# Attention with two feed-forward layers: early weights decoded over ten steps a piece, bias groups behind the steps' own work, first products amid the end

## The chip, the cores and the metric

One core of one Trainium2 chip runs the kernel as one program. The metric is the device time of one execution in microseconds; a kernel's time is the median of its runs. The engines are named as in the profile: PE (TensorE, with PEld for its weight loads), DVE (VectorE), ACT (ScalarE), POOL (GpSimd) and SP, whose queue issues all DMAs of this kernel.

## What is computed

```python
scores = scale * q @ k.T                      # 4 batches, 8 heads, 576 positions, 64 wide
x = (log1p(|i - j|) / log1p(max(i, 1)))[..., None]
scores = scores + (relu(x @ w1 + b1) @ w2)    # a bias per head, from an MLP of 32 hidden units
attn = softmax(scores)                        # with 1e-9 added to the sum
x = attn @ v                                  # reshaped to 2304 tokens x 512
h = x @ w_in; x = (h - tanh(h)) @ w_out       # 512 -> 2048 -> 512
x = (silu(x @ w_gate) * (x @ w_val)) @ w_out2 # 512 -> 1536 -> 512
```

The feed-forward products are exact to more than one pass gives: each operand is split into a high and a low part, and a product is three matmuls (`matmul3`, L681). The weights are given as 8 byte numbers and are decoded on the chip into such a pair.

## The kernel before

**Bias groups.** The bias is made in 36 groups (`bias_rows`, L145): four Relu rows (`bias_hidden`, L127, three on DVE L140 and one on ACT L142, made one group ahead), eight matmuls on PE, one eviction on ACT with a scale, and one DMA to a scratch array in DRAM. When the groups of a span t of 128 positions are done, `bias_load` (L178) reads them back as bias tiles, from a count of groups later on, and at once behind the last group. `GEN0` groups are made first, then `GEN_EACH` at a time while more than `GEN_LATE` are left; so 33 are made ahead of the units, and three in the units' first two steps.

**Units.** A unit is (pair of heads hp, batch b, span t); 16 pairs (hp, b), each of five spans in the order 4, 3, 2, 1, 0, give 80 steps. Step i works on several units at once, and the order of the letters in `FIRST_ORDER` (the first step of a pair), `STEP_ORDER` (the other four) and `END_ORDER` (three steps behind the last unit) is the order of issue on every engine. The letters: L loads of q, k, v on SP; u takes the unit of step i - 3 as the turn; C score matmuls (L302, two PSUM buffers, each freed by S); S the score reduction on DVE (L317, adds the bias tile and finds the maximum); E the exponentials on ACT (L328); N the reciprocals of the sums of unit i - 1 (L337, L338, DVE); M their scaling of the probabilities (L346, POOL); p and P transposes of the turn's probabilities (PE); F and D their copies out of PSUM (F on ACT L394 and L396, D on DVE L394 to L398); V products with v (L413, PE); X and Y the high and low part of x (xh on ACT L422, xl on DVE L428); Q, q, O, o transposes of the next pair's q and k and their copies; H and T the split of q and k (ACT L268, POOL L59); G one bias group.

**End.** `AV_END` gives the step at which the last pair's two groups of value products are issued: behind step 80 all of group 0, behind step 82 all of group 1. Each end step has two turns; behind each end step `aside` (L957) issues one item's hidden products of the first layer (`hidden`, 12 matmuls), and in the second also the first item's pointwise work and the planning of weights.

**Early weights.** A piece of weights is a 512 KB raw tile. While the units run, five pieces are decoded, and two more are begun. Eight operations make one piece, over three rounds: a (L626, DVE), b (L628, DVE), r (L615, ACT) and F (L632, POOL; another F than the copy above) for the piece that is first; m (L619, ACT) and W (L638, DVE, behind it the next raw DMA) for the second; h (L643, ACT) and l (POOL L59) for the third. `ALONE_PARTS` says which are issued in which step of a round: five steps a round, so the last 35 steps hold seven rounds, behind each step's own work.

```python
STEP_ORDER = "LuXYCHGGSTPpNMVFED"
ALONE_PARTS = ("ma", "", "bhW", "rl", "F")
if 0 <= left < 5 * (EARLY_PAIRS + 2):
    weights.part_of_step(-1, (4 - left) % 5)
```

**After the units** come 140 items of the two layers in one loop; item i's hidden products are issued ahead of the output products of item i - 2, with the pointwise work of i on ACT, DVE and POOL between.

Of the kernel before, what the change touches and what calls it, by code (L numbers as in the profile page):

```python
# [17 lines left out]

B, H, S, D = 4, 8, 576, 64
HID = 32  # L20
NT, DM = B * S, H * D
FF1, FF2 = 2048, 1536
# [13 lines left out]
C_B1, C_W2 = C_W1 + 1, C_W1 + 2  # L36
NCONST = C_W2 + QG * H

# [6 lines left out]
    ((6, (0, 1)), (7, (2, 3, 4))),  # L45
    ((9, (0, 1, 2)), (10, (3, 4))),
)
AV_END = {(0, 0): (5, (0, 1, 2, 3, 4)), (1, 0): (7, (0, 1, 2, 3, 4))}

FIRST_ORDER = "LuCpQGGSOPqNMVFoED"  # L50
STEP_ORDER = "LuXYCHGGSTPpNMVFED"
END_ORDER = "NMuPpFDuPpFDVXY"

LAG = 3
GEN_ORDER = [G for t in TORDER for G in range(8 * t, min(8 * t + 8, NG))]
# [6 lines left out]
class Attention:  # L62
# [34 lines left out]
    def bias_setup(self):  # L97
# [17 lines left out]
        for j in range(4):  # L115
            for g in range(QG):
# [3 lines left out]
                )  # L120
        self.scratch = [self.dram.tile([n * H, S], F32, name=f"bias_{t}") for t, (_, n) in enumerate(SPANS)]

# [55 lines left out]
    def bias_load(self, hp, t):  # L178
# [3 lines left out]
        )  # L182
        src = self.scratch[t].rearrange("(q h) k -> q h k", h=H)

# [247 lines left out]
    def run(self, early, aside):  # L432
# [6 lines left out]
        self.ps_qk = {}  # L439
        NP = H // 2  # L440
        units = [(hp, b, t) for hp in range(NP) for b in range(B) for t in TORDER]
# [17 lines left out]
        def gen(n):  # L459
            for _ in range(n):  # L460
                if gens:
                    G = gens.pop(0)
                    self.bias_rows(G)
                    done = NG - len(gens)
                    if not any(x // 8 == G // 8 for x in gens):
                        due.append((G // 8, done + 2))
                    if due and done >= due[0][1]:
                        self.bias_load(0, due.pop(0)[0])
                    if not gens:
                        for t, _ in due:  # L470
                            self.bias_load(0, t)
                        self.gen_ctx.close()
                        early()
# [17 lines left out]
        for n, (hp, b) in enumerate(pairs):  # L491
            for z, when in enumerate(AV_STEPS):
                for after, cs in when:
                    if (hp, b) == pairs[-1]:
                        after, cs = AV_END.get((z, cs[0]), (0, ()))
                    if cs:
# [17 lines left out]
        def transposes(which):  # L514
            return lambda i: i in preps and self.qk_transpose(*preps[i], which)

        at = lambda f, i: f(units[i]) if 0 <= i < len(units) else None
        last = len(units) - 1
# [5 lines left out]
        def next_turn(i):  # L524
# [6 lines left out]
            E=lambda i: at(self.expo, i), V=products, X=lambda i: self.values_high(), Y=lambda i: self.values_low(),  # L531
            Q=transposes("q"), q=transposes("k"), O=lambda i: self.qk_raw("q"), o=lambda i: self.qk_raw("k"),
            H=lambda i: i % 5 and self.qk_high(), T=lambda i: i % 5 and self.qk_low(), G=lambda i: gen(1),
        )
        for i in range(len(units) + 3):
            for a in END_ORDER if i > last else STEP_ORDER if i % 5 else FIRST_ORDER:
                work[a](i)
            if i == len(units) - 1:
                self.ps_ctx.close()
            if i >= len(units):  # L540
                self.values_high()
                self.values_low()
            aside(len(units) - 1 - i)
        self.values_high()
        self.values_low()

# [7 lines left out]
class Weights:  # L554
# [109 lines left out]
    def part_of_step(self, now, n):  # L664

        if n == 0:
            self.plan(now)
        for part in ALONE_PARTS[n]:
            dict(
# [19 lines left out]
SHARED_TWO = dict(s2=("two0", 0), g=("two0", 1), gh=("two1", 0), gl=("two1", 1))  # L689
GROUP1, GROUP2 = 4, 3  # L690
EARLY_PAIRS = 5
BEV_BUFS, GEN0, GEN_LATE, GEN_EACH = 5, 5, 4, 2
RAW_BUFS, POINT_AT = 2, -2
PACED, SOON = 74, 7
ALONE_PARTS = ("ma", "", "bhW", "rl", "F")
UNITS = [(0, 512), (512, 512), (1024, 512), (1536, 512), (2048, 256)]
ORDER, LAST_ORDER = (0, 1, 4, 2, 3), (0, 1, 2, 3, 4)

# [238 lines left out]
@with_exitstack  # L937
def moe_attention_kernel(ctx, tc, q, k, v, packed, w_in, w_out, w_gate, w_val, w_out2, out, dbg=None):
    nc = tc.nc
    xp = ctx.enter_context(tc.tile_pool(name="xp", bufs=1, side="right"))  # L940
    xh = xp.tile([128, 4, NT], F32R, name="xh")
    xl = xp.tile([128, 4, NT], F32R, name="xl")
    shared = ctx.enter_context(tc.tile_pool(name="shared", bufs=1))
    moe = Moe(tc, xh, xl, w_in, w_out, w_gate, w_val, w_out2, out, shared)
    weights = Weights(tc, moe.pieces)
    n1, n = moe.n1, len(moe.items)
    with tc.manual_schedule():
        with ExitStack() as ctx_a:
            moe.constants(shared)
            att = Attention(tc, (q, k, v, packed), xh, xl, shared)  # L950

            def early():
                weights.tmp_pools(ctx, "right")
                weights.pools(ctx, EARLY_PAIRS, "right")
                weights.load()

            def aside(left):  # L957

                if 0 <= left < 5 * (EARLY_PAIRS + 2):
                    weights.part_of_step(-1, (4 - left) % 5)  # L960
                if left < 0:
                    moe.matmuls(-1 - left)
                if left == POINT_AT:
                    weights.plan(0)
                    moe.pointwise(0, weights, True)

            att.pools(ctx_a)
            att.run(early, aside)
        if dbg and "xh" in dbg:
            nc.sync.dma_start(out=dbg["xh"], in_=xh.bitcast(F32))  # L970
            nc.sync.dma_start(out=dbg["xl"], in_=xl.bitcast(F32))
        weights.pools(ctx, 12 - EARLY_PAIRS, "left")
        weights.polite = False
        accp = ctx.enter_context(tc.tile_pool(name="acc", bufs=1))
        acc = accp.tile([128, 4 * NT], F32, name="acc")
        moe.acc = [acc[:, NT * j:NT * j + NT] for j in range(4)]
        moe.acc2 = [acc[:, 512 * j:512 * j + 512] for j in range(NT // 128)]
        moe.pools(ctx)
        held = []
        for i in range(n + 2):  # L980
            if 3 <= i < n:
                moe.matmuls(i)

            now = []
            if i >= 2:
                held.append(i - 2)
                if i >= n or i == 2 or not moe.starts(i - 2) or len(held) > 1:
                    now, held = held, []
            for j in now[:-1]:
                moe.out_matmuls(j)  # L990
            if 1 <= i < n:
                weights.plan(i)
                moe.pointwise(i, weights, i == n - 1)
            for j in now[-1:]:
                moe.out_matmuls(j)
            weights.due(i)
            if dbg and "yh" in dbg and i == n1 + 2:
                nc.sync.dma_start(out=dbg["yh"], in_=xh.bitcast(F32))
                nc.sync.dma_start(out=dbg["yl"], in_=xl.bitcast(F32))
        moe.ps_out.close()  # L1000
        moe.ps_ctx.close()
# [46 lines left out]
```

## Time and profile before

| | |
|---|---|
| median of 3 runs | 1208.5 us (1204.66 to 1209.83) |
| the profiled execution | 1212.27 us |
| its span, first to last instruction | 1210.2 us |
| mean granted clock of TensorE | 0.974 of full |
| busy: PE, DVE, ACT, POOL | 1161.6, 826.1, 701.8, 547.5 us |

The profile is of one execution. Its time was 3.8 us above the median of the runs; 2.1 us of it lie outside the span. All times below are us from the span's start. The bias groups and setup fill it up to 66.6 us, the steps run from there to about 350 us, and the layers from about 360 us to the end. "Idle" in a row of the timeline stands in brackets, with what ended it. The granted clock is a share of full speed: 1.00 is the upper level of 2.4 GHz and 0.5 the lower one of 1.2 GHz, so a mean between them says how long each held.

### The profile page before, as it was taken

What the parts mean: (1) busy time and instruction counts of PE and PEld (TensorE: products, weight loads), DVE (VectorE), ACT (ScalarE), POOL (GpSimd) and SP (SyncE); (2) the same over time, 40 slices, a digit from 0 to 9 for tenths busy, and PEclk for the clock granted to TensorE, in tenths of its full rate; (3) what the DMA queues carried; (4) which work ended last, traced back from release to release, by engine and by line L of the source; (5) the groups of instructions that cost most, each with busy time, mean ns of one, the idle gap of its engine ahead of it and who ended that gap; (6) DMA issues with size and microseconds to landing.
All of it is one profiled execution on the core that took longest, in us unless ns stands there. A gap on an engine that the chain in (4) does not pass through costs nothing.

```text
span 1210.2 us, 20849 instructions
## 1 busy us (share of the span) xinstructions
PE 1161.6 (96%) x7624; PEld 918.7 (76%) x7624; DVE 826.1 (68%) x1620; ACT 701.8 (58%) x1439; POOL 547.5 (45%) x513
## 2 busy tenths in 40 slices
PE   6979999989889999999999999999999999999998
PEld 3456666656657888888888888788888888888887
DVE  6957888777668888989997988853466266434232
ACT  6977888868648888778777787521233124213111
POOL 1035666666635535535544475851344144324111
PEclk9979999988789999999999999999999999999999
DMA  5761525253101211111110110220012012100012
GB/s 153 256 188 35 148 60 149 56 145 88 48 28 53 70 35 53 53 36 35 53 53 18 53 53 18 72 68 1 18 53 88 1 36 70 53 1 18 35 38 85
DMA packets 104694, 77.89 MB, mean 64 GB/s; under 512 B 68624, under 2 KB 89232, under 8 KB 104592
## 3 DMA queue, kind: packets, MB, share of 16 engines
q1 hardware_dynamic: 104592, 76.56, 21.3%
q8 instruction: 60, 0.98, 0.4%
q14 instruction: 42, 0.34, 0.1%
HBM read 61.20 MB, written 15.34 MB: 63 GB/s over the span
## 4 chain that ended last, share of the span: by engine, by line
PE 77%; DVE 9%; ACT 8%; issue 3%; SPq 1%; DMA 1%; POOL 1%; DVEq 0%; ACTq 0%; POOLq 0%
PE y L684 16%; PE h L684 15%; PE val L684 12%; PE o L684 12%; PE gate L684 12%; PE s L302 3%; PE x L413 3%; DVE p L317 3%; ACT p L328 2%; DVE r L140 1%; DVE r L337 1%; DVE pt L394 1%; PE pTa L368 1%; ACT qraw L244 1%; PE pE L381 1%
## 5 line engine op out<-in xcount | busy, mean ns | idle before, releaser
L868 ACT ACTIVATE sq<-gate 128x512 f32<-128x512 f32 (+1 forms) x60 | 33.3, 555 | 328.8 <-PE gate L684 328.8
L59 POOL TENSOR_TENSOR gl<-g,gh 128x512 fp32r<-128x512 f32 (+1 forms) x67 | 82.7, 1235 | 248.6 <-ACT gh L819 187.9
L874 DVE TENSOR_TENSOR sq<-gate,sq 128x512 f32<-128x512 f32 (+1 forms) x60 | 38.2, 637 | 189.8 <-ACT sq L868 189.8
L346 POOL TENSOR_SCALAR p<-p,r 128x576 f32<-128x576 f32 x144 | 113.5, 800 | 73.7 <-ACT p L328 26.7
L684 PE MATMUL y<-gh,whi 128*128 128x512 f32 (+1 forms) x428 | 139.8, 369 | 1.2 <-POOL gh L59 1.2
L317 DVE CUSTOM_DVE_ANT_0 p<-s,bt 128x576 f32<-128x576 f32 x144 | 103.8, 753 | 43.0 <-PE s L302 41.0
L684 PE MATMUL h<-xh,whi 128*128 128x512 f32 (+1 forms) x320 | 118.1, 369 | 0.0
L684 PE MATMUL h<-xl,whi 128*128 128x512 f32 (+1 forms) x320 | 117.9, 368 | 0.0
L684 PE MATMUL h<-xh,wlo 128*128 128x512 f32 (+1 forms) x320 | 117.7, 368 | 0.0
L684 PE MATMUL y<-gh,wlo 128*128 128x512 f32 (+1 forms) x320 | 117.7, 368 | 0.0
L328 ACT ACTIVATE p<-p,m 128x576 f32<-128x576 f32 x144 | 110.8, 771 | 11.4 <-DVE m L317 10.0
L302 PE MATMUL s<-k,q 64*128 64x288 f32 x768 | 82.2, 327 | 23.8 <-DVE m L317 22.6
L684 PE MATMUL o<-whi,gh 128*128 128x512 f32 x288 | 103.6, 389 | 0.0
L302 PEld LDWEIGHTS s<-k,q 64*128 64x128 f32 x768 | 62.2, 197 | 51.7 <-DVE m L317 29.0
L59 POOL TENSOR_TENSOR gh<-g,gh 128x512 fp32r<-128x512 f32 (+1 forms) x33 | 39.5, 1196 | 126.8 <-ACT gh L819 96.7
L684 PEld LDWEIGHTS y<-gh,whi 128*128 128x128 f32 x428 | 79.3, 188 | 15.0 <-POOL gh L59 1.5
L684 PE MATMUL val<-xh,whi 128*128 128x512 f32 (+1 forms) x240 | 88.4, 368 | 1.1 <-DVE g L812 1.1
L413 PE MATMUL x<-pt,vn 128*64 128x256 f32 (+1 forms) x512 | 87.4, 471 | 2.1 <-DVE xl L428 1.1
L684 PE MATMUL gate<-xl,whi 128*128 128x512 f32 (+1 forms) x240 | 88.3, 368 | 0.0
L684 PE MATMUL val<-xh,wlo 128*128 128x512 f32 (+1 forms) x240 | 88.3, 368 | 0.0
L684 PE MATMUL val<-xl,whi 128*128 128x512 f32 (+1 forms) x240 | 88.3, 368 | 0.0
L684 PE MATMUL gate<-xh,wlo 128*128 128x512 f32 (+1 forms) x240 | 88.3, 368 | 0.0
(148 smaller groups left out, 3237.1 us busy)
## 6 DMA issues: line engine op xcount, KB each, us to landing
raw_out<-in_moe_w_out_dram SPq DMA_DIRECT2D x28, 512.0 KB
bias<-bev SPq DMA_DIRECT2D x36, 288.0 KB
raw_in<-in_moe_w_in_dram SPq DMA_DIRECT2D x16, 512.0 KB
raw_gate<-in_moe_w_gate_dram SPq DMA_DIRECT2D x12, 512.0 KB
raw_val<-in_moe_w_val_dram SPq DMA_DIRECT2D x12, 512.0 KB
bt<-bias SPq DMA_DIRECT2D x16, 288.0 KB
out_dram<-acc SPq DMA_DIRECT2D x18, 256.0 KB
qn<-in_q_dram SPq DMA_DIRECT2D x32, 128.0 KB
```

The source lines that it names most:

```text
L59: nc.gpsimd.tensor_tensor(out, a, b, ALU.subtract)
L140: nc.vector.tensor_scalar(r, src, b1, 0.0, ALU.add, ALU.max)
L244: nc.scalar.activation(self.qraw[:, 0:512].rearrange("p (h n) -> p h n", h=2), ps[:, :, 0:256], AF.Copy, scale=-0.125,)
L302: nc.tensor.matmul(self.st[u][j][:, e, 0:HALF], lhs, k[r, y, e * HALF:(e + 1) * HALF], start=n == 0, stop=n == 2,)
L317: nc.vector.tensor_tensor_reduce(out=p[:, n, :].rearrange("p (e f) -> p e f", e=2), in0=ps[n][:, :, 0:HALF], in1=bt[:, n, :].rearrange("p ...
L328: nc.scalar.activation(p[:, n, :], p[:, n, :], AF.Exp, bias=m[:, n:n + 1], scale=-1.0, accum_out=ls[:, n:n + 1],)
L337: nc.vector.tensor_scalar(r[:, 0:ng], ls[:, 0:ng], 1e-9, None, ALU.add)
L346: nc.gpsimd.tensor_scalar(p[:, n, :], p[:, n, :], r[:, n:n + 1], 1.0, ALU.mult, ALU.mult)
L413: nc.tensor.matmul(ps[r, 0:n], lhs, rhs, start=c == 0, stop=c == 4)
L684: nc.tensor.matmul(out, lhs[a], rhs[b], start=first and n == 0, stop=last and n == 2)
L868: self.nc.scalar.activation(self.tmp(it, "sq"), it["p"][0], AF.Sigmoid)
L874: nc.vector.tensor_tensor(it["sq"], gate, it["sq"], ALU.mult)
```

## The change

Groups ahead of the units: 31 instead of 33 (`GEN_LATE` 6), so steps 0 and 1 make two each and step 2 one. In the first steps the groups G come behind S and the split or copies of q and k. In all steps N and M come behind V, F and D. A round of decoding takes ten steps, so the last 70 steps hold the seven rounds, and the parts stand in other steps. In the end steps `aside` is issued between the two turns instead of behind everything, and the last pair's group 0 of value products one step later.

```diff
-AV_END = {(0, 0): (5, (0, 1, 2, 3, 4)), (1, 0): (7, (0, 1, 2, 3, 4))}
-
-FIRST_ORDER = "LuCpQGGSOPqNMVFoED"
-STEP_ORDER = "LuXYCHGGSTPpNMVFED"
-END_ORDER = "NMuPpFDuPpFDVXY"
+AV_END = {(0, 0): (6, (0, 1, 2, 3, 4)), (1, 0): (7, (0, 1, 2, 3, 4))}
+
+FIRST_ORDER = "LuCpQSOGPqVFoGDNME"
+STEP_ORDER = "LuXYCHSTGGPpVFDNME"
+END_ORDER = "NMuPpFDAuPpFDVXY"
...
+            A=lambda i: aside(last - i),
...
-            aside(len(units) - 1 - i)
+            if i <= last:
+                aside(last - i)
...
-BEV_BUFS, GEN0, GEN_LATE, GEN_EACH = 5, 5, 4, 2
+BEV_BUFS, GEN0, GEN_LATE, GEN_EACH = 5, 5, 6, 2
...
-ALONE_PARTS = ("ma", "", "bhW", "rl", "F")
+ALONE_PARTS = ("a", "", "h", "ml", "W", "b", "", "r", "F", "")
...
-                if 0 <= left < 5 * (EARLY_PAIRS + 2):
-                    weights.part_of_step(-1, (4 - left) % 5)
+                n = len(ALONE_PARTS)
+                if 0 <= left < n * (EARLY_PAIRS + 2):
+                    weights.part_of_step(-1, (n - 1 - left) % n)
```

## Rows read from the trace of the kernel before

**Rows 1.** Windows from S to S: a plain pair, two decoding pairs, all six.

```profile
core 0: us, PE busy (x) PEld busy (x) DVE busy (x) ACT busy (x) POOL busy (x), PEclk, DMA share, GB/s
150.70:166.48 15.78, 14.95 (x191) 10.74 (x191) 12.87 (x41) 13.07 (x33) 10.05 (x14) 1.00 0.26 59
213.83:231.68 17.85, 16.36 (x191) 11.86 (x190) 13.86 (x42) 13.64 (x34) 11.61 (x15) 0.90 0.23 52
312.18:332.66 20.48, 18.02 (x192) 12.79 (x191) 15.04 (x44) 14.72 (x36) 13.65 (x15) 0.83 0.15 42
213.83:332.66 118.83, 105.02 (x1142) 74.38 (x1141) 87.88 (x258) 86.84 (x213) 79.02 (x89) 0.86 0.32 86
```

**Rows 2.** Timeline of PE (start, us): fourth scores in a plain and two decoding pairs.

```profile
177.25 0.40 PE L302 MATMUL s<-k,q 64*128 64x288 f32 x1 [0.56 <-DVE m L317]
177.93 1.06 PE L302 MATMUL s<-k,q 64*128 64x288 f32 x11 [0.28 <-DVE m L317]
...
225.25 0.40 PE L302 MATMUL s<-k,q 64*128 64x288 f32 x1 [1.21 <-DVE m L317]
225.93 1.62 PE L302 MATMUL s<-k,q 64*128 64x288 f32 x11 [0.28 <-DVE m L317]
...
283.89 0.39 PE L302 MATMUL s<-k,q 64*128 64x288 f32 x1 [1.97 <-DVE m L317]
```

**Rows 3.** Timeline of DVE in a plain pair.

```profile
169.84 0.42 DVE L428 TENSOR_TENSOR xl<-x,xh 128x256 fp32r<-128x256 f32 x1 [1.43 <-ACT xh L422]
...
174.28 0.85 DVE L337 TENSOR_SCALAR r<-l 128x2 f32<-128x2 f32 x1
...
176.03 0.48 DVE L428 TENSOR_TENSOR xl<-x,xh 128x320 fp32r<-128x320 f32 x1
...
182.26 0.76 DVE L317 CUSTOM_DVE_ANT_0 p<-s,bt 128x576 f32<-128x576 f32 x1 [0.85 <-PE s L302]
```

**Rows 4.** Groups of instructions in the six decoding pairs: b, W, r, h.

```profile
line engine op names shapes xcount | busy us, mean ns | idle before us <-releasers
...
L628 DVE SCALAR_TENSOR_TENSOR bits_in<-raw_in,bits_in 128x512 int32<-128x512 int32 x4 | 3.0, 754 | 0.0
...
L638 DVE SCALAR_TENSOR_TENSOR bits_in<-m_in,bits_in 128x512 f32<-128x512 f32 x4 | 2.7, 677 | 0.0
L615 ACT ACTIVATE r_in<-raw_in 128x512 int32<-128x512 uint32 x4 | 2.7, 672 | 0.0
...
L643 ACT CAST whi<-bits_in 128x512 fp32r<-128x512 f32 x3 | 1.8, 608 | 0.0
```

**Rows 5.** Timelines of POOL and DVE: M and a, at one time.

```profile
292.97 1.65 POOL L346 TENSOR_SCALAR p<-p,r 128x576 f32<-128x576 f32 x2 [2.15 <-ACT qraw L244]
...
293.57 0.42 DVE L626 TENSOR_SCALAR bits_in<-raw_in 128x512 int32<-128x512 int32 x1
```

**Rows 6.** Timeline of ACT in the plain pair: xh, and the copy behind step 3.

```profile
175.52 0.41 ACT L422 CAST xh<-x 128x320 fp32r<-128x320 f32 x1
...
179.54 0.59 ACT L394 COPY pt<-pTa 128x512 f32<-128x512 f32 x1 [0.60 <-PE pTb L368]
```

**Rows 7.** Timeline of POOL: split of k, and two M beside b and W.

```profile
173.69 1.41 POOL L59 TENSOR_TENSOR k<-kraw,k 128x576 fp32r<-128x576 f32 x1 [0.29 <-ACT k L268]
...
301.31 2.42 POOL L346 TENSOR_SCALAR p<-p,r 128x576 f32<-128x576 f32 x2 [0.39 <-DVE r L338]
```

**Rows 8.** Windows: the opening, up to the first S.

```profile
0.00:66.56 66.56, 55.75 (x592) 25.34 (x592) 51.73 (x114) 50.98 (x79) 5.36 (x13) 1.00 0.67 211
```

**Rows 9.** Timeline of SP: last load of step 1, write of the last group.

```profile
74.59 0.61 SPq L219 DMA_DIRECT2D qkn<-in_k_dram  x1
75.30 0.53 SPq L176 DMA_DIRECT2D bias<-bev  x1
```

**Rows 10.** Timeline of DVE: S of step 4, second head.

```profile
82.04 0.76 DVE L317 CUSTOM_DVE_ANT_0 p<-s,bt 128x576 f32<-128x576 f32 x1 [0.53 <-DMA bt<-bias]
```

**Rows 11.** Windows: last unit's scores to last value product.

```profile
345.10:368.76 23.66, 21.58 (x152) 12.97 (x150) 11.69 (x25) 9.18 (x18) 6.24 (x8) 0.78 0.03 6
```

**Rows 12.** Timeline of PE: third item's products, second item's low part.

```profile
368.69 0.50 PE L684 MATMUL h<-xh,whi 128*128 128x512 f32 x1
...
378.13 0.50 PE L684 MATMUL y<-gl,whi 128*128 128x512 f32 x1 [0.75 <-POOL gl L59]
```

## The prediction

> **What bounds it now.** I read the timeline first, for the starts of VectorE's score reduction (L317, written S here). There are 80 steps, five to a pair, so the S starts cut the attention stage into pairs; then I read the windows pair by pair. Without weight decoding a pair takes 15.78 us, TensorE is busy for 14.95 of it and its clock is granted in full; the six pairs that decode early weights and lie wholly in the stage take 118.83 us [rows 1]. Six plain pairs would be 94.68 us, so decoding costs 24.15 us. The reader should see two things in these rows: the mean clock falls to 0.90 in the first such pair (17.85 us) and to 0.83 later (20.48 us), and no engine is near full in them (VectorE 15.04 of 20.48). So delay and clock are paid, not throughput.
>
> Next I read what TensorE waits for. In a plain pair it stands before the fourth step's second score product, because S of step 3 frees that PSUM: 0.56 us, then 0.28 us for the second head. In the first decoding pair the first of these waits is 1.21 us, later 1.97 us [rows 2]. The first decoding pair has the waits 1.21 + 0.28 = 1.49 us and its clock fell to the lower level of 1.2 GHz for a while; 0.56 + 0.28 = 0.84 us never made it fall in the plain pairs. What a fall costs: 17.85 - 15.78 = 2.07, less the longer wait 1.21 - 0.56 = 0.65, is 1.4 us. In the last full pair, 20.48 - 15.78 - (1.97 - 0.56) = 3.3 us, which holds all else that decoding delays too. After the attention stage the first layer's products keep TensorE full, so what is saved before them is saved in the whole.
>
> **Decoding over ten steps.** The same eight operations per piece are issued, and the same raw loads on SP (one per piece, behind L638), now twice as far apart; nothing is removed but the bunching. The index of a step in its part list is the step number modulo ten, so a piece takes a pair starting at an even tenth (a at step 0, h at 2, m and l at 3, W at 4) and the one after it (b at 0, r at 2, F at 3). One by one:
>
> a and b lie at the end of step 0. VectorE sits idle there for 1.43 us before xl [rows 3]; a takes 0.42 and b 0.75 [rows 4, 5]: nothing, by that cover. If it went, b would cost its 0.75 in seven pairs. W (0.68) lies at the end of step 4, where VectorE idles for 0.85 us before the next pair's S [rows 3, 4]: nothing, with 0.17 to spare. m is on ScalarE at the end of step 3, where it idles for 0.60 us before the next copy [rows 6]; it costs no more than r's 0.67, so 0.07 at most. l and F are on GpSimd, with 10.05 of 15.78 us busy [rows 1]; behind them stands the scaling M of a unit whose transposes come two steps later: nothing.
>
> h and r are what is left. They stand on ScalarE behind the exponentials of step 2, and behind them the cast xh, which comes at once, without idle time ahead of it [rows 6]. Who waits: xl on VectorE, behind it S of step 3, and for that TensorE's fourth scores. h takes 0.61, r 0.67 [rows 4], less about 0.1 by which neighbours overlap, so xh ends some 0.55 us later. N now stands behind D on VectorE, which takes 0.85 us of N, blocked behind GpSimd's split of k, out of the way ahead of D [rows 3, 7]; but xh (0.41 us from 175.52) was nearly the last to end before xl anyway, so this gives back only some 0.08. I take 0.47 us per pair; bounds 0 and 0.67. It falls in 11 pairs: r in the odd pairs 3 to 13, h in the even pairs 6 to 14 (the last pair prepares no further q and k and has slack on ScalarE). Sum: 5.2 us.
>
> **The clock.** TensorE's two waits in such a pair become 0.84 + 0.47 = 1.31 us. The rows have 0.84 (clock kept) and 1.49 (fell); 1.31 is nearer to the latter, so I expect falls, but not in each pair, as no row decides between the two. I take 5 of 11, at the 1.4 us of the first decoding pair: 7.0 us. Bounds: none, and all eleven. Sum of the middle: 24.15 - 5.2 - 7.0 = 12 us gained.
>
> **N behind D, and a rule against it.** GpSimd's scaling M waits for N, so it comes up to 0.9 us later; its reader comes two steps on: nothing. But a now starts just behind N, so together with M. The rows show a at 0.42 us in the middle of an M [rows 5], two M taking 1.65 us there, and 2.42 us beside b and W [rows 7]. The Trainium skill's page "SBUF — State Buffer", section "SBUF: two separate sides", says that the port pair shared by VectorE and GpSimd is held for a whole instruction and the other one fully blocks. By that rule a would wait out M, and the sum would be some 1.5 us worse (seven times 0.2 us beyond the 1.43 us of cover). The wait of N behind the k split agrees with it, the row of a beside M does not, and I keep the rows.
>
> **Opening.** Two of the 36 bias groups move from ahead of the units into steps 0 to 2. The first S comes at 66.56 us, behind 33 groups and the setup [rows 8], so a group is worth at most 2.0 us there: up to 4.0 earlier. But the last group's rows go out to DRAM and come back as the bias tile of step 4. On SP the write stands behind step 1's q and k loads, is issued at 75.30 us, and S of step 4 gets its tile only at 82.04 [rows 9, 10]: 6.74 us later. After the change the last three groups' writes stand behind those same loads, and the last group is made a step later. So this chain moves little, and the units wait longer for it. I take 0.5 us gained; bounds 4.0 gained, 2.0 lost (one more group's worth of work ahead of the write). The stretch of half clock behind that wait I leave as it is.
>
> **End.** From the last unit's scores to the last attention product TensorE needs 23.66 us, is busy for 21.58 and has a mean clock of 0.78 [rows 11], so the lower clock holds in about 10.4 us. At full clock and without waits the same work is 21.58 - 5.2 = 16.4 us. The change puts the first two products h between the transposes, where they fill waits, and the third ahead of the last attention product (2.9 us). That product could so end 16.4 + 2.9 = 19.3 us on, 4.4 us earlier. Then ScalarE and VectorE have to do the second item's pointwise work behind the last xh and xl; the first product on its low part comes 9.44 us behind the last attention product, after a wait of 0.75 [rows 12]. This chain is not shortened, so TensorE, with one product less to do there, waits some 3.6 us: no loss, as the chain already set the time. The first pointwise work, now ahead of the third-last group's xh and xl on ScalarE and VectorE, has the third h for cover. I take 3 us, as one more stretch of low clock is likely; bounds 4.4 gained, 2 lost (the new wait lowers the clock).
>
> **Sum.** 0.5 + 12 + 3 = 15.5 us. The profiled execution took 1212.3 us, so 1196.8; the runs' median is 3.8 lower, 1208.5, so 1193.
>
> **Rivals.** *The clock holds*: the waits of 1.31 us do not lower it. For it: they are the shorter; against it: 1.49 did. Middle 24.15 - 5.2 = 19.0; time 1208.5 - 22.5 = 1186. *It falls in all eleven pairs* at 1.4 us: middle 3.6, time 1201.5. For it: over all six decoding pairs of before the mean clock is 0.86 [rows 1], no better than in the first, 0.90. *It falls dearly in all eleven*, at up to 3.3 us, as in the last full pair: 5.2 + 36.3 = 41.5 against 24.15, so 17.4 lost, and with opening and end the time is 1222, slower. It decides at (24.15 + 3.5 - 5.2) / 11 = 2.0 us a pair. For it: ten steps mean twice as many pairs with a disturbed wait; against it: that wait is 1.31, not 1.97 + 0.28. *The edges fail*: opening and end lose 2 us each, so 1208.5 - 12 + 4 = 1200.5.
>
> **Chances.** Forecast 0.45, clock holds 0.22, falls in all 0.18, edges fail 0.07, dear falls 0.08. The range 1183 to 1206 takes in the first four with some room for the unknown costs, and leaves the dear falls out. About 0.5% (6 us) is what a measurement can tell from no change: faster than 1202.5 is nearly all of the first four but a third of "falls in all" and of the edges, 0.78; same 0.14; slower 0.08.
>
> **What would show it.** Pairs from the fourth on of about 16.2 us, 17.7 where the clock fell; waits of about 1.0 and 0.28 us before the fourth scores; idle time of VectorE before S of step 4 on the bias tile, longer than before; the last attention product about 20.5 us behind the last scores, and a wait of some 3 us for the second item's low part. Wrong if most pairs are above 18 us, if h and r do not lengthen TensorE's wait, or if the bias tile comes 3 us earlier.

## The result and the profile after

The changed kernel takes 1190.1 us (median of 4 runs, 1188.61 to 1191.62), the kernel before 1208.4 us beside it; the ratio is 0.9854, with a 95% interval of 0.9828 to 0.9880. The profiled execution took 1191.62 us, with a span of 1189.8 us: 20.4 us less than the span before. Cut at the starts of the score reductions S, the difference lies in three places: 2.7 us up to the first S of the third pair (103.34 before, 100.62 after), 14.4 us in pairs 2 to 14 (counted from 0; 229.32 and 214.90 us), 3.3 us behind that (877.56 and 874.31 us).

The windows of the kernel after answer to [rows 1]; in order, a pair with neither h nor r, one with r, one with h in which the clock fell, and pairs 2 to 14 together:

```profile
core 0: us, PE busy (x) PEld busy (x) DVE busy (x) ACT busy (x) POOL busy (x), PEclk, DMA share, GB/s
132.58:148.31 15.73, 14.89 (x191) 10.76 (x191) 13.39 (x43) 13.59 (x34) 10.62 (x14) 1.00 0.69 190
148.31:164.53 16.22, 14.89 (x191) 10.76 (x190) 13.54 (x41) 13.64 (x34) 11.26 (x15) 1.00 0.28 63
164.53:182.31 17.78, 16.50 (x191) 11.52 (x190) 13.85 (x42) 14.11 (x35) 12.94 (x16) 0.90 0.33 81
100.62:315.52 214.90, 198.63 (x2471) 141.93 (x2470) 176.63 (x539) 179.20 (x446) 148.46 (x182) 0.98 0.41 105
```

The same 13 pairs before, in the window of that kernel:

```profile
103.34:332.66 229.32, 209.65 (x2472) 149.58 (x2471) 177.96 (x538) 178.36 (x444) 149.44 (x180) 0.93 0.37 96
```

VectorE's and ScalarE's work is the same in both (177.96 and 176.63, 178.36 and 179.20 us busy), and TensorE's mean clock rose from 0.93 to 0.98. So nothing was saved in work; delays and low clock went. TensorE's timeline shows the waits of [rows 2] in the same three pairs:

```profile
143.35 0.40 PE L302 MATMUL s<-k,q 64*128 64x288 f32 x1 [0.56 <-DVE m L317]
144.03 1.05 PE L302 MATMUL s<-k,q 64*128 64x288 f32 x11 [0.28 <-DVE m L317]
...
159.57 0.39 PE L302 MATMUL s<-k,q 64*128 64x288 f32 x1 [1.05 <-DVE m L317]
...
175.74 0.40 PE L302 MATMUL s<-k,q 64*128 64x288 f32 x1 [1.00 <-DVE m L317]
```

The wait is 0.56 us without h or r; with one of them it is 0.99 to 1.06 us, in all eleven pairs. It is made on ScalarE and VectorE, as the timelines of the third of these pairs show: h (L645 in this kernel) stands directly ahead of xh, which [rows 6] show without idle time before it, and xl on VectorE now waits, where [rows 3] have no wait. N is short here (0.16 us for the 0.85 of [rows 3]).

```profile
173.56 0.61 ACT L645 CAST whi<-bits_in 128x512 fp32r<-128x512 f32 x1
174.07 0.42 ACT L422 CAST xh<-x 128x320 fp32r<-128x320 f32 x1
```

```profile
173.13 0.16 DVE L337 TENSOR_SCALAR r<-l 128x2 f32<-128x2 f32 x1
...
174.52 0.49 DVE L428 TENSOR_TENSOR xl<-x,xh 128x320 fp32r<-128x320 f32 x1 [1.04 <-ACT xh L422]
174.93 0.75 DVE L317 CUSTOM_DVE_ANT_0 p<-s,bt 128x576 f32<-128x576 f32 x1
```

In the opening, the first S comes at 60.45 us instead of 66.56. The timelines of SP and VectorE answer to [rows 9, 10]: the nine loads on SP start earlier, so the writes behind them do (the last of the three is issued at 73.70 us), and S of step 4 still stands waiting for its bias tile, now for 3.37 us. The last row is that S in the kernel before, which waited 1.41 us.

```profile
71.90 0.61 SPq L219 DMA_DIRECT2D qkn<-in_k_dram  x1
72.61 1.51 SPq L176 DMA_DIRECT2D bias<-bev  x3
76.49 1.27 SPq L188 DMA_DIRECT2D bt<-bias  x3
```

```profile
79.59 0.76 DVE L317 CUSTOM_DVE_ANT_0 p<-s,bt 128x576 f32<-128x576 f32 x1 [3.37 <-DMA bt<-bias]
```

```profile
80.75 0.76 DVE L317 CUSTOM_DVE_ANT_0 p<-s,bt 128x576 f32<-128x576 f32 x1 [1.41 <-DMA bt<-bias]
```

At the end, the window from the last S to the last attention product answers to [rows 11], the timeline row below it to the second of [rows 12]: the second item's first low-part product starts 30.14 us behind that S (327.63 us), where it was 33.12 us (345.01 to 378.13).

```profile
327.63:349.29 21.66, 21.26 (x165) 13.80 (x160) 11.47 (x26) 9.08 (x19) 8.18 (x9) 0.92 0.08 25
```

```profile
357.77 0.50 PE L686 MATMUL y<-gl,whi 128*128 128x512 f32 x1 [0.92 <-POOL gl L59]
```

### The profile page after: what moved, and what is told of

It reads as the page before. It is cut to its first block, busy times and chain, and to the rows that moved or that the text cites. A ratio compares the mean times of both kernels' runs of the same rounds, so it can differ in the third digit from the quotient of the medians.

```text
span 1189.8 us, 20849 instructions
## 1 busy us (share of the span) xinstructions
PE 1145.6 (96%) x7624; PEld 907.9 (76%) x7624; DVE 824.2 (69%) x1620; ACT 701.4 (59%) x1441; POOL 544.0 (46%) x513
## 3 DMA queue, kind: packets, MB, share of 16 engines
q1 hardware_dynamic: 104592, 76.56, 21.7%
## 4 chain that ended last, share of the span: by engine, by line
PE 79%; ACT 10%; DVE 4%; issue 3%; DMA 2%; SPq 1%; POOL 1%; ACTq 0%; DVEq 0%; POOLq 0%
PE h L686 16%; PE y L686 16%; PE val L686 12%; PE o L686 12%; PE gate L686 12%; ACT p L328 4%; PE s L302 3%; PE x L413 3%; DVE p L317 2%; DMA bias<-bev 1%; PE pTa L368 1%; DVE r L140 1%; PE pE L381 1%; ACT xh L422 1%; ACT k L268 1%
## 5 line engine op out<-in xcount | busy, mean ns | idle before, releaser
L346 POOL TENSOR_SCALAR p<-p,r 128x576 f32<-128x576 f32 x144 | 109.7, 774 | 86.5 <-PE s L302 37.0
L317 DVE CUSTOM_DVE_ANT_0 p<-s,bt 128x576 f32<-128x576 f32 x144 | 103.8, 753 | 21.7 <-PE s L302 17.0
L302 PE MATMUL s<-k,q 64*128 64x288 f32 x768 | 76.9, 314 | 19.6 <-DVE m L317 18.8
L302 PEld LDWEIGHTS s<-k,q 64*128 64x128 f32 x768 | 57.7, 186 | 46.5 <-DVE m L317 32.0
L686 PE MATMUL gate<-xh,whi 128*128 128x512 f32 (+1 forms) x240 | 88.2, 368 | 0.0
```

Source lines behind the costliest of these rows:

```text
L302: nc.tensor.matmul(self.st[u][j][:, e, 0:HALF], lhs, k[r, y, e * HALF:(e + 1) * HALF], start=n == 0, stop=n == 2,)
L317: nc.vector.tensor_tensor_reduce(out=p[:, n, :].rearrange("p (e f) -> p e f", e=2), in0=ps[n][:, :, 0:HALF], in1=bt[:, n, :].rearrange("p ...
L346: nc.gpsimd.tensor_scalar(p[:, n, :], p[:, n, :], r[:, n:n + 1], 1.0, ALU.mult, ALU.mult)
L686: nc.tensor.matmul(out, lhs[a], rhs[b], start=first and n == 0, stop=last and n == 2)
```

## Experiments

The theory: h and r, each ahead of xh, lengthen TensorE's wait by some 0.5 us in eleven pairs; the clock falls in some of these; the rest of the decoding is hidden. The rivals: the new order of N and M carries the gain, or decoding's load delays the pairs wherever it stands. Each run was timed beside runs of the kernel before on its own chip, whose medians there were 1204.0 to 1206.1 us (1208.4 beside the kernel after), so ratios are what to compare, and differences of medians between kernels that were timed on different chips are rough. A "fall" is a stretch at the lower clock within pairs 2 to 14.

**e1_decode_only: only the ten-step decoding.**

```diff
-ALONE_PARTS = ("ma", "", "bhW", "rl", "F")
+ALONE_PARTS = ("a", "", "h", "ml", "W", "b", "", "r", "F", "")
```

(With it the code in `aside` that takes the step modulo ten.)

> The kernel before with the ten-step decoding alone. Theory (the spread of the decoding carries most of the gain: 0.5 us of delay in eleven pairs and a few falls of the clock instead of 24 us): 12 to 15 us below the kernel before, about 1195 us; pairs of 15.8 and 16.3 us, with three to six of about 17.7 us; the wait ahead of the fourth scores is about 1.05 us in eleven pairs. Rival (the new order of N and M carries it, the spread alone moves the delays only): within 3 us of the kernel before.

Measured: 1197.3 us, ratio 0.9932 (0.9909 to 0.9955), a gain of 7.7 us, which neither theory had. In its profile the waits are as expected (0.99 to 1.06 us in the eleven pairs), and the clock fell five times, within the three to six expected; pairs 2 to 14 took 219.58 us, 4.7 more than in the kernel after. Its span, 1196.3 us, is 13.9 below that of the profile of before, as the theory had it; but that profile, at 1212.3 us and a clock of 0.974, is slower than all fifteen runs of the same kernel on this chip (1202.7 to 1208.9 us, clock 0.977 to 0.983). So the time that the old decoding costs in the profile of before is more than it usually costs: e2_end_only, with the same decoding, took 226.31 us in pairs 2 to 14 for the 229.32.

**e2_end_only: only the new end.**

```diff
-AV_END = {(0, 0): (5, (0, 1, 2, 3, 4)), (1, 0): (7, (0, 1, 2, 3, 4))}
+AV_END = {(0, 0): (6, (0, 1, 2, 3, 4)), (1, 0): (7, (0, 1, 2, 3, 4))}
-END_ORDER = "NMuPpFDuPpFDVXY"
+END_ORDER = "NMuPpFDAuPpFDVXY"
```

(With it the calls of `aside` as in the change.)

> The kernel before with the new end alone (products of the first items between the turns, group 0 one step later). Theory: about 3 us below the kernel before, 1205.5 us, the second item's first low-part product 30 us behind the last unit's score reduction instead of 33. Rival (the chain of pointwise work sets the end whatever stands ahead of it, so the products only move): within 1 us of the kernel before.

Measured: 1203.7 us, ratio 0.9996 (0.9978 to 1.0014), and runs from 1201.7 to 1209.2 us. The rival's number. Yet in the profiled execution the stretch behind the last S took 862.3 us, 2.9 less than in the profile of before. Its run at 1201.7 us had a mean clock of 0.982, that at 1209.2 us 0.977: low clock goes with a spread of the runs that is more than the end is worth. That is taken up below (e8_old_end).

**e3_opening_only: only the opening.**

```diff
-BEV_BUFS, GEN0, GEN_LATE, GEN_EACH = 5, 5, 4, 2
+BEV_BUFS, GEN0, GEN_LATE, GEN_EACH = 5, 5, 6, 2
-FIRST_ORDER = "LuCpQGGSOPqNMVFoED"
-STEP_ORDER = "LuXYCHGGSTPpNMVFED"
+FIRST_ORDER = "LuCpQSOGPqNMVFoGED"
+STEP_ORDER = "LuXYCHSTGGPpNMVFED"
```

> The kernel before with 31 groups ahead of the units and the groups behind S in the first steps, N and M where they were. Theory (the chain of the last group through DRAM sets the opening, and it starts about 1 us earlier since the loads ahead of it on SP start earlier): 1.5 to 3 us below the kernel before, the first S about 6 us earlier, S of step 4 only 1 to 1.5 us earlier. Rival (the opening's gain belongs to the groups saved ahead of the units): 4 us or more.

Measured: 1201.7 us, ratio 0.9974 (0.9958 to 0.9991), a gain of 3.3 us between the two numbers expected. The profile decides: the first S comes at 60.75 us, 5.8 us earlier than before, S of step 4 at 79.50, 1.25 earlier, the theory's picture. The units' earlier begin is not what counts.

**e4_norm_early: the kernel after with N and M back ahead of V, F and D.**

```diff
-STEP_ORDER = "LuXYCHSTGGPpVFDNME"
+STEP_ORDER = "LuXYCHSTGGPpNMVFED"
```

(`FIRST_ORDER` likewise.)

> The kernel after with N and M back ahead of V, F and D. Theory (N behind D is hidden either way, because xh and not VectorE is last ahead of xl): within 1.5 us of the kernel after, 1189 to 1192 us, with N of 0.85 us in step 2 again. Rival (the blocked N was on the path in each pair): 0.7 us for each of the 16 pairs, so 11 us above the kernel after, about 1201 us.

Measured: 1194.7 us, ratio 0.9910 (0.9894 to 0.9926); 4.5 us above the kernel after (0.6%, or 6.8 us, by the ratios), so neither number. In the profiles pairs 2 to 14 are 4.6 us longer. Pairs without a fall are 0.05 us longer than in the kernel after (15.78 and 16.27 us for 15.73 and 16.22), even ones from the fourth on some 0.2 (16.63 for 16.45); e9_norm_early_late_hr, where nothing falls, puts that at 1.4 us in sum. The rest is the clock, which fell five times here and three times there. Windows of pairs 2 to 14 in this kernel:

```profile
100.50:320.02 219.52, 203.21 (x2472) 144.03 (x2472) 184.83 (x540) 179.67 (x446) 150.76 (x181) 0.96 0.40 102
```

The clock's mean is 0.96 against 0.98.

**e5_h_r_late: h and r where ScalarE idles, l and F behind them.**

```diff
-ALONE_PARTS = ("a", "", "h", "ml", "W", "b", "", "r", "F", "")
+ALONE_PARTS = ("a", "", "", "m", "Wh", "b", "", "", "rl", "F")
```

> The kernel after with the parts of a round as a | - | - | m | W, h | b | - | - | r, l | F: h and r no longer ahead of xh, but at the end of steps 4 and 3, where ScalarE idles 1.13 and 0.60 us. Theory (h and r ahead of xh are the whole delay, and through TensorE's wait of 1.05 us they make the clock fall): every pair takes 15.8 us, the wait is 0.56 us everywhere, the clock does not fall between pairs 2 and 14, and the time is 8 to 10 us below the kernel after, about 1181 us. Rival (the decoding's load on VectorE and GpSimd delays the pairs wherever it stands): less than 3 us below the kernel after, and pairs of 16.2 us.

Measured: 1179.6 us, ratio 0.9783 (0.9751 to 0.9815), 10.5 us below the kernel after (8.6 by the ratios; 10.3 in pairs 2 to 14 of the profiles). These pairs take 15.73 to 15.75 us each, every wait before the fourth scores is 0.55 or 0.56 us, and the clock never falls:

```profile
98.45:303.01 204.56, 193.68 (x2471) 139.94 (x2470) 177.31 (x539) 178.71 (x446) 145.66 (x180) 1.00 0.43 109
```

The same decoding, with the same busy times, costs nothing at all in these places, so the rival (decoding's load) is out. What the ten-step decoding cost was where its parts stood, directly and through the clock: h and r ahead of xh in the main. But the edit moves l and F too, since they need h and r, and l had a small price of its own ("Decoding" below).

**e6_h_r_together: h and r in the same step.**

```diff
-ALONE_PARTS = ("a", "", "h", "ml", "W", "b", "", "r", "F", "")
+ALONE_PARTS = ("a", "", "rh", "ml", "W", "b", "", "", "F", "")
```

> The kernel after with r moved next to h, both at the end of step 2 of the even pairs. Theory (the length of TensorE's wait decides whether the clock can fall): from the seventh pair on the even pairs wait 1.5 to 1.6 us and fall more often, in four or more of the five, while the odd ones wait 0.56 us, take 15.8 us and never fall; the delay in sum is the same, the time within 4 us of the kernel after. Rival (falls come with the number of disturbed pairs, not with the length of the wait): fewer falls than the kernel after, one or two, and 2 us or more below it.

Measured: 1192.3 us, ratio 0.9885 (0.9849 to 0.9921). Four of the five even pairs with both parts fell, none of the odd ones, and none of the two with r alone. Windows of pair 8 and pair 9, and TensorE's waits in both:

```profile
198.42:216.65 18.23, 16.39 (x191) 11.75 (x191) 13.66 (x43) 14.61 (x36) 12.79 (x16) 0.91 0.61 175
216.65:232.39 15.74, 14.90 (x191) 10.78 (x191) 13.61 (x42) 13.07 (x33) 10.27 (x14) 1.00 0.26 58
```

```profile
210.19 0.40 PE L302 MATMUL s<-k,q 64*128 64x288 f32 x1 [1.55 <-DVE m L317]
210.87 1.37 PE L302 MATMUL s<-k,q 64*128 64x288 f32 x11 [0.28 <-DVE m L317]
...
227.42 0.39 PE L302 MATMUL s<-k,q 64*128 64x288 f32 x1 [0.56 <-DVE m L317]
```

Seven disturbed pairs had four falls where the kernel after had three in eleven, so the rival is out. Falls go with the length of the wait: 1.55 us fell in 4 of 5, 0.98 to 1.12 us in 18 of the 46 pairs of all profiles that have it, 0.56 us in none of 87.

**e7_gen_late_4: 33 groups ahead of the units, the new order kept.**

```diff
-BEV_BUFS, GEN0, GEN_LATE, GEN_EACH = 5, 5, 6, 2
+BEV_BUFS, GEN0, GEN_LATE, GEN_EACH = 5, 5, 4, 2
```

> The kernel after with 33 groups ahead of the units again, the new order in the steps kept. Theory (the last group's way through DRAM to the bias tile of step 4 sets the opening): the first S about 2.7 us later than in the kernel after, but S of step 4 within 1 us of it or earlier, since one group less stands in the steps; the time within 1.5 us of the kernel after. Rival (what counts is when the units begin): 2.7 us above the kernel after.

Measured: 1191.3 us, ratio 0.9882 (0.9840 to 0.9923): not told apart from the kernel after. S of step 4 starts at 79.81 us (79.59 after), as the theory has it. Why it isn't earlier stands on ScalarE and SP: the last group's eviction ends at 70.54 us, three us earlier than in the kernel after, but its write stands behind the last of the loads.

```profile
70.23 0.31 ACT L174 ACTIVATE bev<-bpsx,nipsi 128x64 f32<-128x64 f32 x1
```

```profile
73.71 0.61 SPq L219 DMA_DIRECT2D qkn<-in_k_dram  x1
74.42 0.53 SPq L176 DMA_DIRECT2D bias<-bev  x1
76.71 1.28 SPq L188 DMA_DIRECT2D bt<-bias  x3
```

Its four runs lie between 1187.5 and 1196.2 us; the profiled one, the slowest, has five falls in the eleven pairs, at the waits of the kernel after and with N behind D as there.

The next three runs stand on e5_h_r_late, where no pair falls, so that a few us can be seen. They were timed on another chip than it, and the interval of each ratio overlaps that of e5_h_r_late, so what an edit is worth is read from the profiles.

**e8_old_end: e5_h_r_late with the end of the kernel before.**

```diff
-AV_END = {(0, 0): (6, (0, 1, 2, 3, 4)), (1, 0): (7, (0, 1, 2, 3, 4))}
-END_ORDER = "NMuPpFDAuPpFDVXY"
+AV_END = {(0, 0): (5, (0, 1, 2, 3, 4)), (1, 0): (7, (0, 1, 2, 3, 4))}
+END_ORDER = "NMuPpFDuPpFDVXY"
```

> The kernel of e5_h_r_late with the end of the kernel before (aside behind each end step, group 0 one step earlier). Theory (the chain of pointwise work behind the last attention product sets the end; what the profile of before lost there was a second stretch of low clock that not each execution has): 0 to 1.5 us above e5_h_r_late, the stretch from S of step 79 to the end of the span 861.5 to 862.5 us against 861.7. Rival (the products amid the end save 3 us, as forecast): 2.5 us or more above it, 864.5 us or more.

Measured: 1182.9 us, ratio 0.9812 (0.9796 to 0.9827), 3.3 us above e5_h_r_late, and 865.9 us behind the last S, 4.3 more than there: the rival's numbers. (The four runs of either kernel come in two levels some 3 us apart, 1181.6 and 1184.5 us here, 1178.2 and 1181.0 there, so the difference is the same at both; what parts the levels is open.) What the old end loses is seen in the same 4.2 us of work in both kernels, from 2.87 us behind the last S; first in e8_old_end, then in e5_h_r_late:

```profile
316.80:321.00 4.20, 0.83 (x11) 0.51 (x10) 2.33 (x6) 0.59 (x1) 3.38 (x4) 1.00 0.01 2
```

```profile
317.60:321.80 4.20, 3.48 (x22) 2.58 (x22) 2.37 (x6) 0.59 (x1) 3.38 (x4) 1.00 0.01 2
```

VectorE, ScalarE and GpSimd do the same; N takes 1.22 and 1.25 us there, beside a two-input step of the decoding on GpSimd. TensorE waits for the copy behind that N. With the old end it has nothing else to do (0.83 us busy of 4.20), waits 2.48 us and goes on at the lower clock; with the new end it runs the moved products (3.48 us busy), waits 0.72 and keeps the upper clock. The timeline of TensorE in e8_old_end, and in e5_h_r_late:

```profile
320.76 0.27 PE L368 MATMUL pTb<-ident,p 64*128 64x64 f32 x1 [2.48 <-DVE pt L394]
```

```profile
321.59 0.28 PE L368 MATMUL pTb<-ident,p 64*128 64x64 f32 x1 [0.72 <-DVE pt L394]
```

The old end does not always lose: the stretch behind the last S takes 861.8 us in e1_decode_only and 862.6 in e3_opening_only, as with the new end (860.8 to 862.3 us in the eight profiles that have it), for 865.2 in the kernel before and 865.9 here. The two that lost are the two whose clock fell 7.5 and 7.8 us behind the last S, for 6.83 us; no profile with the new end has that. A long wait alone does not decide it, as the longest in the kernel before until then is 0.60 us, and e3_opening_only, with the same order of work there, did not fall. So the new end is worth some 3 to 4 us where the clock falls there in the old one, and nothing elsewhere; when it does is open.

**e9_norm_early_late_hr: e5_h_r_late with N and M ahead of V, F and D.**

```diff
-STEP_ORDER = "LuXYCHSTGGPpVFDNME"
+STEP_ORDER = "LuXYCHSTGGPpNMVFED"
```

> The kernel of e5_h_r_late with N and M ahead of V, F and D. Theory (N behind D is worth 0.05 us a pair directly; what e4_norm_early lost beyond that was falls of the clock, and here the waits are too short for any): 0.5 to 1.2 us above e5_h_r_late, pairs of 15.78 us, no fall between pairs 2 and 14. Rival (N behind D saves time of its own): 3 us or more above it, or falls in the pairs.

Measured: 1181.1 us, ratio 0.9798 (0.9785 to 0.9812), 1.4 us above e5_h_r_late. Pairs are 15.78 us, the even ones from the eighth on 15.95 to 15.99; pairs 2 to 14 take 205.94 us against 204.56, and no wait is longer than 0.56 us, no fall among them. So N behind D is worth 1.4 us of its own, and what the pairs of e4_norm_early lost beyond that came through falls.

**e10_bias_by_act: e5_h_r_late with 33 groups ahead, the late groups' rows written from ScalarE's queue.**

```diff
-        nc.sync.dma_start(out=self.scratch[t][128 * r0:128 * r0 + 128, :], in_=out)
+        (nc.scalar if both is None else nc.sync).dma_start(out=self.scratch[t][128 * r0:128 * r0 + 128, :], in_=out)
...
-BEV_BUFS, GEN0, GEN_LATE, GEN_EACH = 5, 5, 6, 2
+BEV_BUFS, GEN0, GEN_LATE, GEN_EACH = 5, 5, 4, 2
```

> The kernel of e5_h_r_late with 33 groups ahead of the units, and the three groups in the steps written to DRAM by DMAs issued from ScalarE's queue, right behind their eviction, instead of from SP behind step 1's eight loads. Theory (the way of the last group to the bias tile of step 4 sets the opening, and the loads stand in that way): S of step 4 about 76.5 us instead of 79.0, the low clock behind it shorter or gone, 2.5 to 6 us below e5_h_r_late. Rival (the two transfers themselves are what takes the time, not the queue): S of step 4 at 79 us or later, within 1 us of e5_h_r_late.

Measured: 1176.3 us, ratio 0.9753 (0.9739 to 0.9766), 3.3 us below e5_h_r_late (1.8 in the spans of the profiles) and 13.8 us below the kernel after: the fastest kernel of this study. The write is issued at 71.59 us, right behind the eviction, and the read 2.7 us later. Timelines of ScalarE and SP:

```profile
71.25 0.31 ACT L174 ACTIVATE bev<-bpsx,nipsi 128x64 f32<-128x64 f32 x1
71.59 0.33 ACTq L176 DMA_DIRECT2D bias<-bev  x1
```

```profile
71.29 0.61 SPq L219 DMA_DIRECT2D qkn<-in_k_dram  x1
74.25 1.27 SPq L188 DMA_DIRECT2D bt<-bias  x3
```

S of step 4 starts at 77.45 us instead of 79.00, 0.95 later than forecast. It still waits 0.30 us for the second head's tile, and a stretch of low clock in the first pairs is left.

## Why the prediction was right, point by point

The range held the time (1190.1 in 1183 to 1206), and the likeliest case was the one that came: delays in eleven pairs and falls in some of them. The sum was 15.5 us, the medians differ by 18.2 and the profiled spans by 20.4. There is luck in how near that is: the costs were taken from a profile of before with more low clock than most of its other runs have, and three falls were fewer than the same waits had in other kernels.

**Decoding.** h and r at 0.47 us in 11 pairs: measured 0.49 with r (16.22 - 15.73), in just those pairs. TensorE's wait was to be 1.31 us in sum, and is 1.34 at most (1.06 + 0.28). Nothing for a, b, W, m, l and F: right for all but l and W together. The even pairs with h in which the clock holds take 16.45 us (pairs 8 and 10), 0.72 over 15.73: 0.44 is the wait, the other 0.28 comes at the pair's end, which pair 4, with W but without l, does not lose. There N, now behind D, is held by l on GpSimd until 214.27 us, W ends behind it, and the next pair's S (the last row below) starts without the idle time that was W's cover. So "W ... nothing, with 0.17 to spare" did not hold beside l. The delays come to 6.5 us for the 5.2. VectorE and GpSimd at the end of pair 8:

```profile
213.55 0.72 DVE L337 TENSOR_SCALAR r<-l 128x2 f32<-128x2 f32 x1
214.30 0.17 DVE L338 RECIPROCAL r<-r 128x2 f32<-128x2 f32 x1
214.38 0.67 DVE L640 SCALAR_TENSOR_TENSOR bits_in<-m_in,bits_in 128x512 f32<-128x512 f32 x1
214.97 0.75 DVE L317 CUSTOM_DVE_ANT_0 p<-s,bt 128x576 f32<-128x576 f32 x1
```

```profile
212.96 1.28 POOL L59 TENSOR_TENSOR wlo<-bits_in,whi 128x512 fp32r<-128x512 f32 x1
```

**The clock.** Five falls of 1.4 us: three of 1.3 us (17.74 to 17.78 for the 16.45 of even pairs without one), 3.9 us for the 7.0. The middle gained 14.4 us for 12. The size was off by the number of falls, for which the prediction said that no row decides, and none did: profiles with the same waits had three (after) and five (e1_decode_only, e4_norm_early, e7_gen_late_4). Why those had more is open.

**N behind D.** Costed at nothing, with 0.08 us given back: 0.05 us a pair in the trace, 1.4 us in e9_norm_early_late_hr. By medians e4_norm_early lost 4.5 us, the rest of it through two more falls; whether N ahead of D brings these is not shown, as e7_gen_late_4, with N behind D, had five as well. That a beside M costs nothing held, but not by the row that was read for it: [rows 5] merge two M, of 0.75 and 0.93 us, and a started 0.15 us before the end of the first. Where a starts earlier within an M it is held up: it ends 0.28 us behind that M, and so takes 0.43 us when 0.15 us of the M are left, 0.52 at 0.24 and 0.71 at 0.43. The first two rows below, of M and a in the last full pair before, are of the last kind. In the kernel after it starts 0.15 to 0.28 us ahead of the M in all seven pairs, and takes 0.41 to 0.43. The exclusive hold that the Trainium skill states ("SBUF — State Buffer", section "SBUF: two separate sides") agrees with all of these; keeping [rows 5] against it was the misreading. It agrees for N too, which takes 0.70 us beside l and 0.16 without it.

```profile
313.71 0.75 POOL L346 TENSOR_SCALAR p<-p,r 128x576 f32<-128x576 f32 x1 [2.47 <-PE kT L233]
...
314.02 0.71 DVE L626 TENSOR_SCALAR bits_out<-raw_out 128x512 int32<-128x512 int32 x1
```

The rows of a and N in pair 6 of the kernel after:

```profile
166.65 0.41 DVE L628 TENSOR_SCALAR bits_in<-raw_in 128x512 int32<-128x512 int32 x1
...
179.55 0.70 DVE L337 TENSOR_SCALAR r<-l 128x2 f32<-128x2 f32 x1
```

**Opening.** Forecast 0.5 us, measured 1.2 us up to S of step 4 and 2.7 us up to the third pair. The mechanism was right (first S 6.1 us earlier, most of it lost in the longer wait for the bias tile). What was too small is "So this chain moves little": the loads ahead of the writes move with the units, so the last write was issued at 73.70 us, 1.6 earlier. The rest is the low clock behind the wait, which "I leave as it is": it was 13.65 us long before and 10.24 after, and with the same opening 6.8 in e5_h_r_late and 13.7 in e6_h_r_together. What sets it is open, so that part is chance.

**End.** Forecast 3 us, measured 3.0 in these two profiles, and the last attention product 21.7 us behind the last S for the 20.5 said. But of these 3.0 us 2.8 are busy time: the windows up to the second item's low part hold 190 products of TensorE in 30.29 us before and in 27.50 after, while its waits in them are as long in sum (2.83 and 2.64). So the term is the lower clock, a second stretch of 6.83 us that this profile of before has and that of the kernel after has not, and the waits that the new end fills come back behind it, as the sum said: the 3 us expected for the low part are spread over three places (0.93, 0.40 and 0.92 us). These windows, of the kernel before and then of the one after:

```profile
345.01:378.13 33.12, 30.29 (x190) 19.86 (x188) 20.02 (x37) 18.23 (x36) 11.50 (x13) 0.85 0.11 32
```

```profile
327.63:357.77 30.14, 27.50 (x190) 18.42 (x185) 18.75 (x37) 17.51 (x35) 10.80 (x12) 0.94 0.11 36
```

The old end alone is no fixed loss (e1_decode_only, and e3_opening_only with the very steps of before), which the prediction did not see, and which fits that e2_end_only measured next to nothing. That the number came out is luck in part: the prediction read the low clock of one execution as the old end's own.

## What to carry to other kernels

The side job of this case, spread over more steps, cost time only where it stood ahead of an instruction that the bound engine waits for; look for the idle time of each engine step by step and put every part there, as moving h and r, with l and F behind them, was worth 10.3 us in pairs 2 to 14. Before costing a wait in front of TensorE by its length, see whether the clock fell behind longer waits of the kind: a disturbed pair of the kernel after cost 0.7 us where it held and 2.0 where it fell. One profile may hold more low clock than most runs; take such a cost from several. A transfer on a chain shares its queue with all that is issued ahead of it, so try a write that something waits for on a queue that is free at that moment: S of step 4 came 1.55 us earlier by it.

## What the runs showed of the hardware

A wait of TensorE of 0.98 to 1.12 us (and 0.28 behind it) was followed by the lower clock in some pairs and not in others of the same kernel, one of 0.56 us never. Over pairs 2 to 14 of all twelve profiles the low clock began in none of 87 pairs with a wait of 0.54 to 0.56 us, in 18 of 46 with 0.98 to 1.12, in 2 of 3 with 1.21 or 1.22, in 4 of 5 with 1.54 to 1.56 and in 14 of 15 with 1.95 to 1.98. The first fall in the kernel after, for one, begins 2.4 us behind the end of a wait of 1.00 us, and TensorE is busy without idle time while it lasts.

```profile
178.18:181.59 3.41, 3.41 (x16) 1.90 (x16) 2.83 (x7) 1.89 (x5) 2.99 (x4) 0.50 0.50 154
```

Two short VectorE instructions, when they start while GpSimd is within one of its own, do not end before that one does. N is 0.16 to 0.17 us alone, 0.70 and 0.85 beside a two-input instruction and 1.22 when it starts just behind one's begin; each time it ends 0.02 to 0.03 us behind it. GpSimd's scaling of one input holds up a, which ends 0.28 us behind it.

The kernel before ran at 1202.7 to 1210.8 us over the chips, with mean clocks of 0.984 to 0.973, the slower runs in the main at the lower ones, a spread of 0.7%. On one chip it ran at 1203.3 to 1207.1 us, where e10_bias_by_act, whose pairs have no fall, ran at 1174.6 to 1177.4. How much of the spread is falls within the pairs is not shown.
